# A linear-attention and mixture-of-experts kernel on one core: the first batch's path, the order of its loads and the table that sets the order of the work are changed

## The chip, the core and the metric

The kernel runs on one core of a Trainium2 chip. A core has TensorE (PE in the profile, PEld for its weight loads), VectorE (DVE), ScalarE (ACT), GpSimd (POOL) and SyncE (SP), which here only issues transfers. Each engine takes its instructions in the order in which they are written, and semaphores make one wait for another. The metric is the time of one execution in microseconds of the device, the median of several runs.

## The reference

For 8 batches, 8 heads, 576 tokens and a head size of 64 in fp32, a linear attention with a normalised output feeds four attention experts; each token uses the two experts with the highest gate.

```python
kv = einsum('bhsd,bhse->bhde', k, v)                       # 64 x 64 for each head
o = einsum('bhsd,bhde->bhse', q, kv)
x = o / sqrt(mean(o * o, -1) + 1e-6) * g_norm              # heads side by side: 576 x 512
logits = x @ w_gate                                        # 4 experts, two are kept
for e in range(4):
    q, k, v = x @ wq[e], x @ wk[e], x @ wv[e]              # 512 -> 64
    a = softmax(causal(q @ k.T / 8))                       # 576 x 576
    out += gate[e] * (a @ v @ wo[e])                       # 64 -> 512
```

## The kernel before, in words

The eight batches run through the same chain of tasks. A task has a short name and the batch as its first index. `lk`, `lv` and `lq` load k, v and q of a batch: k and v each in two pieces of 640 and 512 KB (batch 0 in four), q in two halves of 576 KB. `kv` are 40 products in four groups of ten (line 374), `kvc` and `kvm` copy and rearrange their result, `qc` turns q on DVE (line 390), `out` are the products with q (line 401, two halves of tokens), `oc` copies them out of PSUM and `sq` squares them. `SS` sums the squares over each head and `L` makes the logits with the unscaled output (both line 426). `ln`, `rs`, `na`, `nb`, `nc` make 1/sqrt of the sums with one Newton step, `pa` to `pd` split that into two bf16 parts, `sp` spreads them over the partitions with eight small products for each half (line 542), and `xm` multiplies, which gives x (line 552). Then `qp` and `kp` project x onto two experts at a time (line 576), `sc` makes scores (594), `exp` and `msk` the softmax's numerators, `v` the values (561), `pv` their product (623), `rc`, `iv`, `osc` scale, `dt` or `ot` transpose, `y` is the last projection (668), `yc` copies it and `st` stores it. Set-up work goes beside this: `lw` loads the weights for q, k, v in six pieces of 256 KB, in rows of 256 bytes, `ws` scales them by g_norm into place, `z` clears pads, `es` makes the matrix that `sp` multiplies with.

The order of all tasks is written out: `ORDER` is a table of two-character codes into the list that `names` makes, `ENGINE` gives the engine or the queue of each task, and `BANKS` its PSUM banks. The main loop (line 709) emits the tasks in that order, so each engine's and each queue's order follows from it. `ZEROS` puts products of zeros ahead of a task (line 704): 8, 2, 3, 2 and 1 of them, up to batch 1. `GATE` has one digit for each load: a digit n other than 0 makes the load wait until the load n places earlier has landed. A load also waits until its buffer is free: k, v and q have two buffers each, so the loads of a batch wait for the products, or for q's turn, two batches earlier. Almost all loads and stores are issued by SP, one after the other; seven of batch 0's ten are issued by ACT.

The order of the tasks sets what PE does between two loads: PE has in hand what the loads up to there allow, and waits at the first task in its list that lacks data.

Of the kernel before, what the change touches and what calls it, by code (L numbers as in the profile page):

```python
# [53 lines left out]
ENGINE = (
    "AVSGSGVVGVVGGGGVGVGGVGVGGGVVVVVVSSSSSSAGAAGVGVGGGVSASASAASAAASAAPPPPAVAVVVVPPAAVGAAAAPPAAGVVAVAVVVVVVVVVVAVGVV"
    "VPPVVVVPVPAPAPAPAPAPAPAPAGGGGPVGVPVGVSPAPVPAPAPAPAGGGGPVVVPVGVSPASPVSPASPVSPVSSSSSSSPPPPAAGVVVVPPAAVAAGVAPPAAV"
    "VVGVAVVVVVVVVVVAVVVVVPPVVVVPAPAPVPVPAPAPAPAPAGGGGPVVVPVGVSPAPAPAPAPAPAGGGGPVVVPVVVSPASPASPASPASPVSSSSSSSPPPPVG"
    "GVVVVPPAGAGAAVGPPAAGVVVVVVVVVVVVVVGAVVVVGPPVVVVPAPVPAPVPAPAPAPAPAGGGGPVGVPVVVSPAPAPAPAPAPAGGGGPVGVPVGVSPVSPASP"
    "ASPASPASSSSSSSPPPPVGVVVVVPPVGAGAAAAPPAAVVVGVVVVVGVVVVVVAVVVVGPPVVVVPAPAPVPAPAPAPAPAPAGGGGPVVVPVVVSPVPAPAPAPAPA"
    "GGGGPVVVPVVVSPASPASPASPVSPVSSSSSSSPPPPAGAVVVVPPVGAGAGVGPPAAGVVGVGVVVVVVVVVVAVVVVGPPVVVVPVPVPAPAPVPAPAPAPAGGGGP"  # L60
    "VGVPVVVSPAPAPAPAPAPAGGGGPVGVPVGVSPVSPASPASPASPASSSSSSSPPPPVVGVVVVPPVGAGAGAGPPAAGVVGVVVVVVVVVVVGAVGVVVPPVVVVPVP"
    "APAPAPAPAPAPAPAGGGGPVGVPVVVSPVPAPAPAPAPAGGGGPVVVPVVVSPASPASPVSPASPVSSSSSSSPPPPVGGVVVVPPVGAGAGAGPPAAVVVVVGVVVVV"
    "VVVVGAVVVVGPPVVVVPVPAPAPVPVPAPAPAPAGGGGPVVVPVVVSPVPAPAPAPAPAGGGGPVGVPVGVSPASPASPASPASPASSSSSSSPPPPAVAVVVVPPVGA"
    "GAGAAPPAAVVVGVGVVVVVVVVVGAVGVVVPPVVVVPAPAPVPVPAPAPAPAPAGGGGPVVVPVVVPVPVPAPAPAPAPAGGGGPVVVPVVVPVPASPVSPASPASPAS"
)
# [684 lines left out]
```

## Time and profile before

| what | value |
|---|---|
| median of 3 runs | 211.37 us (210.36 to 211.82) |
| the profiled execution | 210.57 us |
| its span, from the first to the last instruction | 208.8 us |
| PE busy | 189.7 us (91%), of it 17.1 us products of zeros |
| PEld, DVE, ACT, POOL busy | 147.6, 145.6, 120.5, 82.5 us |
| chain that ended last | PE 68%, DMA 11%, DVE 11%, ACT 4%, issue 3% |
| read from HBM, written | 30.42 MB, 9.44 MB |
| granted TensorE clock, mean | 0.978 |

The profiled execution lies 1.8 us above its span and 0.8 us below the median. PE is busy nearly all the time from the 43rd microsecond on, so what matters is when that state is reached, and whether the loads keep up with it. A busy PE is not a PE at its peak: products that wait for one another inside the engine count as busy.

### The profile page before, as it was taken

What the parts mean: (1) busy time and instruction counts of PE and PEld (TensorE: products, weight loads), DVE (VectorE), ACT (ScalarE), POOL (GpSimd) and SP (SyncE); (2) the same over time, 40 slices, a digit from 0 to 9 for tenths busy, and PEclk for the clock granted to TensorE, in tenths of its full rate; (3) what the DMA queues carried; (4) which work ended last, traced back from release to release, by engine and by line L of the source; (5) the groups of instructions that cost most, each with busy time, mean ns of one, the idle gap of its engine ahead of it and who ended that gap; (6) DMA issues with size and microseconds to landing.
All of it is one profiled execution on the core that took longest, in us unless ns stands there. A gap on an engine that the chain in (4) does not pass through costs nothing.

```text
span 208.8 us, 7252 instructions
## 1 busy us (share of the span) xinstructions
PE 189.7 (91%) x3003; PEld 147.6 (71%) x3018; DVE 145.6 (70%) x368; ACT 120.5 (58%) x206; POOL 82.5 (40%) x184
## 2 busy tenths in 40 slices
PE   7937979599999799999999899999999999999990
PEld 3327456497988587787778688877877888788750
DVE  3023194889769987786997897549986889856660
ACT  2001164954766717665669538657756664789871
POOL 3000053750885822105735550736615252145400
PEclk9995899999999999999999999999999999999997
DMA  5996997999998986859959876601510930353886
GB/s 154 332 374 212 354 161 181 294 173 326 269 337 283 316 289 130 267 189 353 308 159 184 274 250 168 209 8 38 199 36 11 194 91 0 90 153 110 143 296 248
DMA packets 41536, 42.61 MB, mean 204 GB/s; under 512 B 17696, under 2 KB 35104, under 8 KB 41504
## 3 DMA queue, kind: packets, MB, share of 16 engines
q1 hardware_dynamic: 39792, 39.47, 66.7%
q10 hardware_dynamic: 1648, 2.69, 3.7%
q8 instruction: 23, 0.38, 0.7%
q14 instruction: 9, 0.07, 0.1%
q0 software_dynamic: 64, 0.00, 0.1%
HBM read 30.42 MB, written 9.44 MB: 191 GB/s over the span
## 4 chain that ended last, share of the span: by engine, by line
PE 68%; DMA 11%; DVE 11%; ACT 4%; issue 3%; POOL 0%; ACTq 0%; POOLq 0%; DVEq 0%
PE ps L576 14%; PE ps L374 9%; PE ps L594 8%; DMA k_b<-in_k_dram 8%; PE ps L401 7%; PE ps L561 7%; PE ps L426 6%; PE ps L668 6%; PE ps L623 5%; PE ps L704 3%; DMA v_b<-in_v_dram 3%; DVE qT L390 2%; DVE osc L643 2%; PE ps L542 2%; DVE inv L639 1%
## 5 line engine op out<-in xcount | busy, mean ns | idle before, releaser
L605 ACT ACTIVATE PT<-ps 128x1024 bf16<-128x1024 f32 (+1 forms) x64 | 50.9, 835 | 18.4 <-PE ps L594 15.3
L611 POOL TENSOR_SCALAR_AFFINE_SELECT PT<-PT 128x256 bf16<-128x256 bf16 (+1 forms) x80 | 29.2, 387 | 30.2 <-ACT PT L605 29.8
L419 POOL TENSOR_TENSOR sq<-o_sb 128x576 f32<-128x576 f32 x22 | 25.0, 1153 | 32.5 <-DVE jh L310 24.7
L390 DVE STREAM_TRANSPOSE qT<-q_b 128x576 f32<-128x576 f32 x32 | 23.6, 757 | 13.5 <-DMA q_b<-in_q_dram 13.4
L552 DVE TENSOR_TENSOR xT<-o_sb,ps 128x640 fp32r<-128x640 f32 x32 | 24.9, 816 | 3.8 <-PE ps L542 3.5
L374 PE MATMUL ps<-v_b,k_b 128*64 128x64 f32 x640 | 22.9, 232 | 4.7 <-DMA k_b<-in_k_dram 3.6
L374 PEld LDWEIGHTS ps<-v_b,k_b 128*64 128x64 f32 x640 | 21.4, 146 | 7.6 <-DMA k_b<-in_k_dram 3.6
L561 PE MATMUL ps<-wv_r,xT 128*128 128x256 f32 x160 | 23.9, 292 | 0.6 <-DVE osc L643 0.5
L594 PE MATMUL ps<-qTp,kT 64*128 64x64 f32 (+4 forms) x192 | 22.5, 339 | 0.2
L561 PEld LDWEIGHTS ps<-wv_r,xT 128*128 128x128 f32 x160 | 20.4, 188 | 2.7 <-DVE osc L643 0.9
L223 ACT COPY y<-ps 128x512 f32<-128x512 f32 (+1 forms) x29 | 15.7, 559 | 9.6 <-PE ps L668 7.4
L576 PE MATMUL ps<-xT,wq_r 128*128 128x288 f32 x128 | 20.0, 302 | 0.0
L576 PE MATMUL ps<-xT,wk_r 128*128 128x288 f32 x128 | 19.8, 299 | 0.0
L623 PEld LDWEIGHTS <-PT 128*128 128x128 bf16 x480 | 16.7, 97 | 4.4 <-issue 1.2
L704 PE MATMUL ps<-zeros 128*128 128x512 f32 (+1 forms) x32 | 17.1, 677 | 2.7 <-DVE zeros L250 1.1
L223 ACT COPY o_sb<-ps 128x576 f32<-128x576 f32 x22 | 13.5, 638 | 10.2 <-PE ps L401 10.1
L668 PE MATMUL ps<-wo_b,OT 128*128 128x512 bf16 (+1 forms) x81 | 18.3, 343 | 0.6 <-issue 0.2
L623 PE MATMUL ps<-vext,PT 128*128 128x65 bf16 x480 | 18.6, 193 | 0.2
L576 PEld LDWEIGHTS ps<-xT,wq_r 128*128 128x128 f32 x128 | 17.5, 188 | 1.3 <-issue 0.9
L576 PEld LDWEIGHTS ps<-xT,wk_r 128*128 128x128 f32 x128 | 17.7, 188 | 1.0 <-ACT o_sb L223 0.4
L594 PEld LDWEIGHTS ps<-qTp,kT 64*128 64x128 f32 x192 | 14.3, 185 | 5.7 <-issue 2.0
L643 DVE TENSOR_TENSOR osc<-ps,inv 128x256 bf16<-128x256 f32 (+1 forms) x32 | 15.3, 484 | 2.8 <-POOL inv L639 2.2
(110 smaller groups left out, 264.0 us busy)
## 6 DMA issues: line engine op xcount, KB each, us to landing
out_dram<-y SPq DMA_DIRECT2D x32, 256.0 KB, 2.8
q_b<-in_q_dram SPq DMA_DIRECT2D x14, 576.0 KB, 5.8
v_b<-in_v_dram SPq DMA_DIRECT2D x7, 640.0 KB, 7.4
k_b<-in_k_dram SPq DMA_DIRECT2D x7, 640.0 KB, 7.0
k_b<-in_k_dram SPq DMA_DIRECT2D x7, 512.0 KB, 6.5
v_b<-in_v_dram SPq DMA_DIRECT2D x7, 512.0 KB, 5.9
q_b<-in_q_dram ACTq DMA_DIRECT2D x2, 576.0 KB, 7.5
out_dram<-y SPq DMA_DIRECT2D x16, 64.0 KB, 2.1
```

Source lines behind the costliest of these rows:

```text
L223: return nc.scalar.copy(dst, src)
L374: nc.tensor.matmul(p_kv[Dh * t : Dh * t + Dh, j, hh, :], lhsT=kb_[b % NK][:, h, n, :], rhs=vb_[b % NK][:, h, n, :], start=(n == 0), stop=( ...
L390: nc.vector.transpose(qT_[0][:, hh, j * n : (j + 1) * n].rearrange("p j h i -> p (j h i)"), qb_[b % 2][:, hh, j * n : (j + 1) * n, :].rear ...
L419: inst = ew("sq", b, u, p).tensor_tensor(out=dst, in0=src, in1=src, op=mult)
L552: nc.vector.tensor_tensor(out=view(xT_[b % 2]), in0=view(ob_[b % 2]), in1=two("sp", b, u, p)[:, :, 0:320].rearrange("p s (m j) -> p m s j" ...
L561: nc.tensor.matmul(one("v", b, i)[:, n * 256 : (n + 1) * 256], lhsT=xT_[b % 2][:, c, blk * P : (blk + 1) * P], rhs=w_r["v"][:, c].rearrang ...
L576: nc.tensor.matmul(bank_in((nm + "p", b, pr), s)[:, 0:HALF], lhsT=w_r[nm][:, c, 2 * pr : 2 * pr + 2, :].rearrange("p e f -> p (e f)"), rhs ...
L594: nc.tensor.matmul(bank_in(("sc", b, pr, j), el)[:, o : o + hi - lo], lhsT=kT_[(2 * b + pr) % 3][pp, kb * P : (kb + 1) * P], rhs=qTp_[(2 * ...
L605: nc.scalar.activation(PT[:, :, d0 : d0 + o], two("sc", b, pr, j)[:, :, 0:o], ACTF.Exp, scale=scale)
L611: nc.gpsimd.affine_select(out=d, in_=d, compare_op=AluOpType.is_ge, fill=0.0, base=0, pattern=[[0, 2], [1, w]], channel_multiplier=-1)
L623: nc.tensor.matmul(p_O[:, (2 * n + el) * (Hd + 1) : (2 * n + el + 1) * (Hd + 1)], lhsT=PT[:, el, col : col + P], rhs=vx_[b % 2][:, kb, 2 * ...
L668: nc.tensor.matmul(p_y[o * nq : (o + 1) * nq, 0:w], lhsT=OT_[b % 2][:, pr, s0 : s0 + nq], rhs=wo_b[:, pr, o * w : (o + 1) * w], start=(pr ...
```

## The change

Batch 0 gets a path of its own. Its k and v are loaded in two pieces each as in the other batches, its first half of q is the very first load, and its second half comes in two pieces of 288 KB. `sq` of batch 0 reads PSUM on ACT and no longer the copy; its sums `SS` are split into two halves, the second of them `SS2`. `pa` to `pd` are dropped for batch 0: `sp` multiplies the fp32 result of `nc` with a matrix in fp32 that the new task `e32` makes in the buffer `y_[2]`. Of the four `xm` of batch 0 two go to POOL, which reads a copy that the new task `xs` makes on ACT. Only 9 products of zeros are left, ahead of the first `kv`. The loads of g_norm and of the gate's weights become two tasks, issued by ACT. The output of the last two batches is copied into the buffers of k and v, and a store of the last 64 tokens is one transfer, not two. All four tables are new, so the tasks of every batch stand in another order, and many have another engine.

```diff
-ZEROS = {('kv', 0, 0, 0): 8, ('kv', 0, 1, 0): 2, ('out', 0, 1): 3, ('kv', 1, 1, 1): 2, ('out', 1, 1): 1}
+ZEROS = {('kv', 0, 0, 1): 9}
...
-    "01000P0E0v0u0R0U090x0t080A0z0s0B0+17100y0w120-07192z2+131A11141615181C1J1K2-"
...
+    "010A0v0t0D060714130N0P0Q0R050C0U0u0r0s0z020J0S040803000w0x152w0E160I0-"
...
 GATE = (
-    "440006650500463600435646400660633303055345542523520320300236"
+    "000000065544044055564506006553456430300023036240420420606"
 )
...
+    def e32():
+        for a in range(2):
+            ew("e32").tensor_scalar(
+                out=esel_f[:, :, a, :], in0=jj[:, 4 * a : 4 * a + 4, 0].unsqueeze(2).to_broadcast([P, NCH, Dh]),
+                scalar1=-0.5, scalar2=None, op0=mult,
+            )
...
-    def lq(b, hh):
-        return queue("lq", b, hh).dma_start(
-            qb_[b % 2][:, hh].rearrange("p j d -> p (j d)"), q[b, 4 * hh : 4 * hh + 4].rearrange("g (i j) d -> (g i) (j d)", j=NJ)
+    def lq(b, hh, *half):
+        js = slice(half[0] * NJ // 2, (half[0] + 1) * NJ // 2) if half else slice(0, NJ)
...
     def square(b, u, p):
+        if b == 0:
+            src = two("out", b, u, p)[:, :, 0:HALF].rearrange("p c (j i) -> p c i j", j=NJ)
+            dst = sq_[0][:, 2 * p : 2 * p + 2, u * HALF : (u + 1) * HALF].rearrange("p c (i j) -> p c i j", j=NJ)
+            return other_half(nc.scalar.activation(dst, src, ACTF.Square), ("sq", b, u, p))
...
     def ss_mm(b):
-        sums(("SS", b), w_ss, sq_[0])
+        sums(("SS", b), w_ss, sq_[0], range(NCH if b else 2))
+
+    def ss_rest(b):
+        sums(("SS", b), w_ss, sq_[0], range(2, NCH))
...
-                    lhsT=esel[rows, c].rearrange("p a d -> p (a d)"),
-                    rhs=flat(rb["rc"][b % 2])[rows], start=True, stop=True, skip_group_check=True, tile_position=(32 * s, 0),
+                    lhsT=(esel if b else esel_f)[rows, c].rearrange("p a d -> p (a d)"),
+                    rhs=flat(rb["rc"][b % 2] if b else ssl["rstd"][b % 2])[rows], start=True, stop=True, skip_group_check=True, tile_position=(32 * s, 0),
...
+        spread_r = two("sp", b, u, p)[:, :, 0:320] if b or not p else sp_copy(u)
+        ew("xm", b, u, p).tensor_tensor(
+            out=view(xT_[b % 2]), in0=view(ob_[b % 2]), in1=spread_r.rearrange("p s (m j) -> p m s j", j=32), op=mult
+        )
+
+    def sp_copy(u):
+        return sq_[0][:, 2 * u : 2 * u + 2, 0:320]
+
+    def xs(_, u):
+        nc.scalar.copy(sp_copy(u), two("sp", 0, u, 1)[:, :, 0:320])
...
     def y_copy(b, i):
-        y_of[b, i] = y_[y_next[0] % NY]
-        y_next[0] += 1
+        if b >= B - NK:
+            t = (vb_, kb_)[b - B + NK][(B - NK) % NK]
+            y_of[b, i] = t[:].rearrange("p h j d -> p (h j d)")[:, i * D : (i + 1) * D]
...
```

What the tables do is read from the instructions in their order. The head of PE's list, before (zeros are line 704, `kv` line 374, `out` line 401):

```order
L704 MATMUL ps<-zeros 128x512 x8
L374 MATMUL ps<-v_b_81,k_b_79 64x64 x10
L704 MATMUL ps<-zeros 128x256 x2
L374 MATMUL ps<-v_b_81,k_b_79 64x64 x30
L704 MATMUL ps<-zeros 128x512 x3
L401 MATMUL ps<-qT_89,kvs_85 64x288 x8
L401 MATMUL ps<-qT_89,kvx_87 64x288 x8
L401 MATMUL ps<-qT_89,kvs_85 64x288 x8
```

and now (zeros line 734, `kv` 386, `out` 413, `SS`, `SS2` and `L` 442, `sp` 561, `kp` and `qp` 601; v_b_81 and k_b_79 are the buffers of batch 0, v_b_82 and k_b_80 those of batch 1):

```order
L734 MATMUL ps<-zeros 128x512 x9
L386 MATMUL ps<-v_b_81,k_b_79 64x64 x40
L413 MATMUL ps<-qT_89,kvs_85 64x288 x8
L413 MATMUL ps<-qT_89,kvx_87 64x288 x8
L413 MATMUL ps<-qT_89,kvs_85 64x288 x8
L413 MATMUL ps<-qT_89,kvx_87 64x288 x8
L442 MATMUL ps<-sq_92,w_ss 32x160 x16
L442 MATMUL ps<-o_sb_90,wg 32x160 x16
L561 MATMUL ps<-rstd_95,y_154 128x160 x16
L386 MATMUL ps<-v_b_82,k_b_80 64x64 x40
L601 MATMUL ps<-xT_133,wk_r 128x288 x8
L601 MATMUL ps<-xT_133,wq_r 128x288 x8
```

Before, the products of zeros stand between the groups of batch 0, and batch 1's `kv`, `out`, `SS` and `L` stand ahead of the first projection; now batch 0 goes through to `sp` first, then `kv` of batch 1, and the projections `kp` and `qp` of two experts follow at once, ahead of `out` of batch 1.

The head of SP's list of loads, before (v_b0, k_b0, q_b0 are the buffers of batch 0, those with a 1 of batch 1, PT0 to PT2 hold the weights; the other loads of batch 0 are on ACT's queue):

```order
L352 DMA v_b0_81<-in_v_dram 64x4x256 x2
L352 DMA k_b0_79<-in_k_dram 64x4x320
L352 DMA v_b1_82<-in_v_dram 64x8x320
L352 DMA k_b1_80<-in_k_dram 64x8x256
L352 DMA v_b1_82<-in_v_dram 64x8x256
L352 DMA k_b1_80<-in_k_dram 64x8x320
L364 DMA q_b1_84<-in_q_dram 128x1152 x2
L256 DMA wg_in_65<-in_moe_w_gate_dram 64x4x4
L253 DMA g8_64<-in_g_norm_dram 64x1
L352 DMA k_b0_79<-in_k_dram 64x8x320
L328 DMA PT1_144<-in_moe_wk_dram 64x16x64
L328 DMA PT0_143<-in_moe_wq_dram 64x16x64 x2
```

and now (the two pieces of k of batch 0 are on ACT's queue):

```order
L375 DMA q_b0_83<-in_q_dram 128x1152
L362 DMA v_b0_81<-in_v_dram 64x8x256
L362 DMA v_b0_81<-in_v_dram 64x8x320
L375 DMA q_b0_83<-in_q_dram 128x576 x2
L362 DMA v_b1_82<-in_v_dram 64x8x256
L375 DMA q_b1_84<-in_q_dram 128x1152
L362 DMA k_b1_80<-in_k_dram 64x8x320
L338 DMA PT1_144<-in_moe_wk_dram 64x16x64
L362 DMA v_b1_82<-in_v_dram 64x8x320
L362 DMA k_b1_80<-in_k_dram 64x8x256
L338 DMA PT0_143<-in_moe_wq_dram 64x16x64
L375 DMA q_b1_84<-in_q_dram 128x1152
```

Before, SP's first three pieces are of batch 0 and the next ones of batch 1; now all of batch 0 stands first, and weights for k and q stand among the loads of batch 1. The list goes on in both with batch 2, the weights for v, and batches 3 and 4.

## Rows read from the trace of the kernel before

**Rows 1.** The chain of waits that ended last, first 45 us (start and length in us, what ran; "DMA" is a transfer that was waited for, x the number of records).

```profile
2.74 6.67 DMA v_b<-in_v_dram
9.48 6.06 DMA k_b<-in_k_dram
...
16.50 3.48 PE ps L374 x60
20.00 0.38 ACT kvs L223
20.43 3.70 PE ps L704 x6
24.13 1.24 PE ps L401 x32
...
27.32 1.99 PE ps L704 x4
29.32 2.48 PE ps L374 x80
31.80 1.22 PE ps L426 x32
...
40.36 2.38 PE ps L426 x64
42.74 3.38 PE ps L576 x24
```

**Rows 2.** The timeline of the first products of zeros (start and length in us, engine, line, operation, shapes; PE are the products, PEld their weight loads, one for each record).

```profile
1.12 9.12 PE L704 MATMUL ps<-zeros 128*128 128x512 f32 x16 [1.12 <-DVE zeros L250]
...
5.34 0.19 PEld L704 LDWEIGHTS ps<-zeros 128*128 128x128 f32 x1 [0.30 <-issue]
5.77 0.19 PEld L704 LDWEIGHTS ps<-zeros 128*128 128x128 f32 x1 [0.24 <-issue]
```

**Rows 3.** Busy time of the engines in stretches of the start (us from the span's start, then length, PE, PEld, DVE, ACT, POOL busy with counts, granted clock, mean busy share of the DMA engines, GB/s).

```profile
10.00:15.00 5.00, 2.11 (x25) 1.37 (x24) 1.12 (x5) 0.00 (x0) 0.00 (x0) 1.00 1.06 373
15.00:20.00 5.00, 3.47 (x60) 3.31 (x60) 1.44 (x2) 0.00 (x0) 0.00 (x0) 0.54 0.66 204
20.00:25.00 5.00, 4.57 (x38) 2.16 (x46) 1.28 (x4) 0.96 (x3) 0.00 (x0) 0.78 1.03 372
...
30.00:35.00 5.00, 5.00 (x128) 3.70 (x132) 2.20 (x6) 1.70 (x5) 1.46 (x5) 1.00 0.59 112
```

**Rows 4.** The same view in longer stretches, up to the landing of the last piece of k of batch 4 (79.34 us).

```profile
2.74:20.00 17.26, 12.84 (x99) 7.59 (x97) 3.04 (x8) 0.00 (x0) 0.00 (x0) 0.87 0.90 301
20.00:60.00 40.00, 36.02 (x614) 26.69 (x615) 26.86 (x55) 23.16 (x42) 18.62 (x30) 0.97 0.99 261
60.00:79.34 19.34, 17.59 (x368) 14.56 (x366) 17.99 (x49) 10.77 (x21) 11.79 (x25) 1.00 0.88 291
20.00:50.00 30.00, 26.02 (x462) 18.19 (x462) 20.43 (x45) 16.37 (x32) 12.10 (x21) 0.96 1.00 243
50.00:60.00 10.00, 10.00 (x156) 8.49 (x157) 6.43 (x11) 6.79 (x10) 6.52 (x9) 1.00 0.95 313
```

**Rows 5.** The chain of waits later on: blocks of products, and the two transfers waited for ahead of `kv` of batch 4 (line 374 at 79.48).

```profile
52.73 4.44 PE ps L576 x32
57.17 2.21 PE ps L401 x64
...
68.65 4.95 DMA k_b<-in_k_dram
73.61 5.73 DMA k_b<-in_k_dram
79.48 2.55 PE ps L374 x80
...
90.35 0.54 PE ps L623 x18
...
104.71 2.55 PE ps L561 x20
...
137.73 0.38 PE ps L623 x12
```

**Rows 6.** The timeline of ACT and DVE in the normalisation of batch 0: a square, then `ln`, `rs`, `nc`, and the last of `pa` to `pd`.

```profile
26.06 0.68 ACT L417 ACTIVATE sq<-o_sb 128x576 f32<-128x576 f32 x1
...
33.09 0.39 ACT L442 ACTIVATE root<-ps,eps_t 128x160 f32<-128x160 f32 x1 [0.22 <-PE ps L426]
...
33.51 0.34 ACT L445 ACTIVATE rstd<-root 128x160 f32<-128x160 f32 x1
...
34.91 0.33 DVE L458 SCALAR_TENSOR_TENSOR rstd<-root,rstd 128x160 f32<-128x160 f32 x1
...
38.07 0.94 DVE L473 SCALAR_TENSOR_TENSOR rc<-rb,m_b,part 128x160 bf16<-128x160 bf16 x1
```

**Rows 7.** Groups of instructions by shape (busy us, mean ns of one, idle time before them and its releasers): the squares on POOL, `xm` on DVE, the scaling of weights on POOL.

```profile
L419 POOL TENSOR_TENSOR sq<-o_sb 128x576 f32<-128x576 f32 x22 | 25.0, 1153 | 32.5 <-DVE jh L310 24.7 <-ACT o_sb L223 7.0 <-DVE o_sb L226 0.8
L552 DVE TENSOR_TENSOR xT<-o_sb,ps 128x640 fp32r<-128x640 f32 x32 | 24.9, 816 | 3.8 <-PE ps L542 3.5 <-ACT wq_r L338 0.2
...
L340 POOL TENSOR_SCALAR wk_r<-PT,g 64x512 fp32r<-64x512 f32 x2 | 3.1, 1562 | 0.2
```

**Rows 8.** The chain of waits: the last copy of an output block ahead of the last stores.

```profile
203.45 0.28 ACT y L223
```

More of the change, by code (lines that the diff above doesn't have):

```diff
@@ L53 @@
+    "EqEwErEsGSGTGsEtExEyEuF0GtH4H5G+EvF1F2H1H6G-H0H2GuGvGxGwGyGzH3"
 )
 ENGINE = (
[L55 to L58, printed above, removed]
@@ L89, in names @@
     for b in range(nb):
-        out += [(m, b, part, par) for part in (r2 if b == 0 else (2,)) for par in r2 for m in ("lk", "lv")]
-        out += [("lq", b, hh) for hh in r2]
+        out += [(m, b, part, par) for part in (2,) for par in r2 for m in ("lk", "lv")]
+        out += [("lq", b, hh) for hh in r2] if b else [("lq", 0, 0), ("lq", 0, 1, 0), ("lq", 0, 1, 1)]
         out += [("kv", b, hh, j) for hh in r2 for j in r2] + [("kvc", b)] + [("kvm", b, t) for t in r2]
@@ L94, in names @@
         out += [("out", b, u) for u in r2] + [(m, b, u, p) for u in r2 for p in r2 for m in ("oc", "sq")]
-        out += [(m, b) for m in ("L", "SS", "ln", "rs", "na", "nb", "nc", "pa", "pb", "pc", "pd", "gm", "gtr", "lg")]
+        out += [] if b else [("SS2", 0), ("xs", 0, 0), ("xs", 0, 1)]
+        out += [(m, b) for m in ("L", "SS", "ln", "rs", "na", "nb", "nc") + (("pa", "pb", "pc", "pd") if b else ()) + ("gm", "gtr", "lg")]
         out += [(m, b) for m in ("g1", "g2", "g3", "g4", "g5", "sh", "ex", "mk", "gt", "den", "rd", "gate")]
@@ L213 @@
     y_ = sbt([P, D], FP32, "y", NY)
+    esel_f = y_[2][:].rearrange("p (c a d) -> p c a d", c=NCH, a=2)
     stage = {
@@ L250, in cz, with cg, cw @@
         nc.vector.memset(zeros[:], 0.0)
-    def cg(hh):
-        queue("cg", hh).dma_start(g8[hh * Dh : (hh + 1) * Dh, :], g_norm.unsqueeze(1))
-    def cw(hh):
-        queue("cw", hh).dma_start(
-            wg_in[hh * Dh : (hh + 1) * Dh], moe_w_gate[hh * D // 2 : (hh + 1) * D // 2, :].rearrange("(c p) e -> p c e", p=Dh)
-        )
+    def cg():
+        queue("cg").dma_start(g8[:], g_norm.unsqueeze(0).unsqueeze(2).to_broadcast([2, Dh, 1]))
+    def cw():
+        for hh in range(2):
+            rows = moe_w_gate[hh * D // 2 : (hh + 1) * D // 2, :].rearrange("(c p) e -> p c e", p=Dh)
+            queue("cw").dma_start(wg_in[hh * Dh : (hh + 1) * Dh], rows)
     def scale_g():
@@ L420, in square, with sums @@
         other_half(inst, ("sq", b, u, p))
-    def sums(key, w, src):
-        for c in range(NCH):
+    def sums(key, w, src, chunks=range(NCH)):
+        for c in chunks:
             for s in range(4):
@@ L683, in store @@
         w = D * nq // P
[L684 to L685 removed]
+        n = P // nq
+        dst = out[b, s0 : s0 + nq, :].rearrange("q (o w) -> o q w", o=n)
+        queue("st", b, i).dma_start(dst, y_of[b, i][:, 0:w])
     emit = dict(
[L688 removed]
+        at=at, cz=cz, cg=cg, cw=cw, g8=scale_g, cs=cs, z=z, wg=wgate, id=ident, idb=idb, j1=j1, j2=j2, es=es, e32=e32, ma=ma, mb=mb,
         lw=lw, ws=ws, lwo=lwo, wo=wo, lk=lk, lv=lv, lq=lq, kv=kv, kvc=kv_copy, kvm=kv_move, qc=q_turn, out=out_mm, oc=o_copy, sq=square,
[L690 to L691 removed]
+        L=l_mm, SS=ss_mm, SS2=ss_rest, ln=ln, rs=rs, na=newton_a, nb=newton_b, nc=newton_c, pa=pa, pb=pb, pc=pc, pd=pd, gm=gm, gtr=gtr,
+        lg=lg, g1=g1, g2=g2, g3=g3, g4=g4, g5=g5, sh=sh, ex=ex, mk=mk, gt=gt, den=den, rd=rd, gate=gate, sp=spread, xs=xs, xm=xm,
         v=v_mm, vc=v_copy, qp=lambda b, pr: proj("q", b, pr), kp=lambda b, pr: proj("k", b, pr),
```

91 lines of the change are left out of this document (46 added, 45 removed).

## The prediction

> **What bounds the kernel now.** I read the page's table first: PE is busy 91% of the span, so the question is where the other 9% and the products of zeros lie. The chain of waits tells of the start [rows 1]: two transfers up to 15.54 us, `kv` of batch 0 from 16.50 to 19.98, a copy of 0.38, then 3.70 us of zeros that stand ahead of `out` in PE's list and hold it back, and so on through batch 1's `kv` and sums until the first projection at 42.74. The reader is to see that 42.7 us pass before PE has work without end, and that zeros (3.70, 1.99) stand on that chain themselves.
>
> The second view is the stretches [rows 4]. The DMA engines are busy 0.90, 0.99 and 0.88 of the time up to 79.34 us, where the last piece of k of batch 4 lands. The chain names two transfers of k ahead of `kv` of batch 4, which starts at 79.48 [rows 5]. So up to there the transfers set the pace, though PE finds other work meanwhile (17.6 of 19.3 us busy in the last of these stretches). From 79.48 to the end of the span 129.3 us are left, and PE is their bound.
>
> **The change, part by part: the head.** `kv` of batch 0 needs its k, v and, ahead of them in the list, half of q: 2.95 MB. At a rate of 0.34 MB per us of busy DMA (329 in 50 to 60, 331 in 60 to 79, 352 in 10 to 15 us: GB/s over share [rows 3, 4]) and the share of 0.90 of the first stretch it lands 9.6 us after the first stretch's start at 2.74, at 12.4 us; the bounds are 10.7 at the 373 GB/s of 10 to 15 us and 15.5 as before. The 9 products of zeros don't hold it: 16 records end at 10.24, two more take 0.43 each [rows 2], so 11.1. Then, step by step: `kv` 2.48 to 14.9; its copy 0.38, the rearranging about 0.6 and the rest of a half of `out` about 0.6 (half of its 1.24) to 16.5 [rows 1]; four squares on ACT at 0.68 to 19.2; `SS2`, half of 1.22, to 19.9; `ln` to `nc` 2.15 (33.09 to 35.24) to 22.0 [rows 6]. The way from there to 39.01, the end of `pd`, 3.8 us [rows 6], is gone. No row shows `sp` in fp32: it lies between half of an `SS` (0.61: as many columns and records, four at a time) and the same 16 records one after the other (160 of 512 columns of 0.43, 2.1 in all); I take 0.61, the nearer kind. The copy `xs` costs about 0.7, and POOL's two multiplies 1153 x 640/576 = 1.28 each [rows 7], against 0.82 on DVE: x is whole at about 26.0. Meanwhile PE does `kv` of batch 1, whose loads (6.75 MB, with one of the weights) land at about 24.4; with 2.48 it ends at 26.9. So the first projection starts near 27 us, 15.8 earlier, with 4.6 us of PE work less behind it (`out`, `L`, `SS` of batch 1).
>
> **The transfers.** This is where most of those 15.8 us are lost. The loads of the weights cost more than their bytes: in 20 to 50 us the share was 1.00 and 243 GB/s were moved [rows 4], 7.29 MB or 21.4 us at 0.34; the 8.6 us over are those of the six weight loads, 1.4 each. For `kv` of batch 4 the new list needs k and v of five batches (11.80 MB), q of four (4.72) and the six weights (1.57), 18.09 MB: 53.2 + 8.6 = 61.8 us of busy DMA. The same sum for before, 21.04 MB, gives 70.5; measured were 0.90 x 17.26 + 0.99 x 40 + 0.88 x 19.34 = 72.2. The new gates leave four to six loads in flight in most of this part; the old ones, with 3 in places, went with a share of 0.59 in 30 to 35 us and of 0.66 in 15 to 20 [rows 3]. I take a share of 0.98, near the 0.99 of 20 to 60 us: 63.1 + 2.7 = 65.8 us. The bounds are 1.06 as in 10 to 15 us (61.0) and 0.88 as in 60 to 79 us (72.9).
>
> PE alone would be there sooner: from the first projection to `kv` of batch 4 the list holds about 30 us of products, which gives 57. Half-way stands `v` of batch 0, which needs the last weights: 12.19 MB, 45.4 us of DMA time at that share, landed at 48.1, scaled at 49.7 (1.56 on POOL [rows 7]); PE would reach it at 42.0. From there 14.9 us of products lead to `kv` of batch 4, at 64.6, within a microsecond of the transfers. So nothing in the head costs anything until it is 8 us worse than above: the wait for the loads covers the longer `sp`, POOL's multiplies, and the loads of weights that DVE's `ws` tasks wait for ahead of copies of batch 1.
>
> **What is left then.** The 129.3 us from `kv` of batch 4 on, and what the new list puts behind it: `SS` of batch 3 (1.22), its `out` (2.21), four `pv` (1.84), two blocks of `v` of batch 1 (2.04, 16 of 20 records in 2.55), scores 0.2 [rows 1, 5], together 7.5: 136.8 us. The rest goes together at nothing: six squares fewer on POOL and six more on ACT (6.9 and 4.1 us) lie under PE, which bounds this part; the own buffers for the last outputs and the single stores of 64 tokens lie in the last 5.4 us after 203.45 [rows 8], where they may give or cost 1 us, since five stores of a batch must still go out. DVE, 18.0 of 19.3 us busy in 60 to 79 [rows 4], is next should PE run faster.
>
> The sum: 65.8 + 136.8 = 202.6 of span, and the 1.8 us around it as before, 204.4, against the profiled 210.57. That execution was 0.8 below the median, so **205.2 us** to compare with 211.37.
>
> **A rule against it.** In 15 to 20 us the granted clock was 0.54, so nearly all of it at the level of 1.2 GHz, after PE had been busy 2.11 of the five microseconds before; at 20 to 25 it was 0.78, then 1.00 [rows 3]. Now PE has gaps in its head and no zeros to fill them. The Trainium skill (TensorE: Matmul & The Clock Gate, section Why this matters for your kernels) warns that idle gaps between bursts of matmuls send the array back to its lower clock; by that rule the sum would be the third rival's. The trace agrees that the clock falls, and shows that it came back while the engine was kept waiting now and then; I keep 205.2.
>
> **Rivals.** First, more: the DMA engines stay as busy as in 10 to 15 us, 1.06, and `kv` of batch 4 starts at 61.0; then 200.4. Against it: before had no more than 0.99 over 20 to 60. Second, little: the transfers gain nothing by their new order, because loads still wait for buffers that PE frees late and the share stays at the 0.90 of the first stretch: 68.7 + 2.7 = 71.4, then 210.8. For it: before reached 0.88 in 60 to 79 us with its gates of 3, and the new gates have 3 there too. Third, slower: the clock. A record of `kv` took 58 ns in 16.5 to 20 us (3.48 for 60) and 31 at the full clock (2.48 for 80) [rows 1], 1.87 times as long. Were PE at 1.2 GHz from the end of the first `kv` to `v` of batch 0, 23.4 us of products (`out` to `kv` of batch 1 8.3, then 15.1) would take 20.4 more: `v` starts at 62.4 and not 49.7, and the end is 12.7 later, 217.9. It decides from 7.7 us added on (the cover), and makes the kernel slower by over 1% from 16 us on, that is 18 us of work at half clock. Against it: in 30 to 35 us the clock was 1.00 [rows 3].
>
> **The numbers.** Chances: forecast 0.58 (its own range 202 to 208.5), more 0.12, little 0.20, clock 0.10. A measurement of this kernel tells about 1% from no change, so faster is below 209.3 and slower above 213.5. The forecast and the first rival are faster; of the second 0.07 are, 0.11 are the same and 0.02 slower; the third is slower: 0.77, 0.11, 0.12. The range of 199 to 212 leaves out the clock and the ends of the first two rivals, about 2 in 10.
>
> **What would show it.** In the new profile: the first projection near 27 us; a DMA share near 0.98 from 5 us to 60; PE waiting for transfers ahead of `kv` of batch 2, `v` of batch 0 or `kv` of batches 3 and 4, the last near 66; from there 137 us to the end with PE busy as before. I am wrong if the clock stands at its lower level for more than a few microseconds after 15 us, if the share stays near 0.9, or if PE, after `kv` of batch 4, waits for other engines where it did not before.

## The result and the profile after

The changed kernel takes 214.39 us, median of 20 runs (211.72 to 217.11); the kernel before, on the same chips, 211.31 (210.36 to 216.23). The ratio is 1.010, interval 1.007 to 1.013: slower by 1%, where 205.2 us was forecast. Ratios are taken without the slow executions, those over 1.5% above the quickest of their kernel (here 8 of the 20), and so this one lies below the quotient of the two medians, 1.015. The profiled execution is the quickest of the twenty, 211.72 us, with a span of 210.0; the spread of the others comes up again below.

The chain of waits of the changed kernel, its first 50 us, answers to [rows 1] (line 386 is `kv`, 601 the projections, 413 `out`, 586 `v`):

```profile
2.86 11.08 DMA g<-in_g_norm_dram
...
14.12 0.79 DVE qT L402 x2
...
17.41 8.18 DMA k_b<-in_k_dram
...
25.72 4.07 PE ps L386 x80
29.79 2.55 PE ps L601 x16
32.34 1.26 PE ps L413 x32
...
34.41 9.03 DMA q_b<-in_q_dram
...
48.26 1.64 PE ps L586 x12
```

The first projection starts at 29.79 us instead of 42.74, and `v` of batch 0 at 48.26. The stretches answer to [rows 3, 4]:

```profile
20.00:25.00 5.00, 2.31 (x60) 1.73 (x52) 3.91 (x8) 2.71 (x5) 1.35 (x1) 1.00 1.17 263
25.00:30.00 5.00, 4.28 (x82) 4.19 (x83) 1.34 (x3) 0.89 (x2) 1.93 (x3) 0.66 1.14 193
30.00:35.00 5.00, 5.00 (x84) 3.85 (x84) 3.41 (x6) 3.65 (x7) 4.32 (x6) 1.00 1.00 304
```

```profile
2.74:20.00 17.26, 15.60 (x205) 8.68 (x207) 6.95 (x18) 5.08 (x10) 5.21 (x16) 1.00 1.06 329
20.00:60.00 40.00, 34.70 (x668) 28.39 (x661) 27.06 (x63) 23.63 (x40) 15.90 (x26) 0.96 1.06 292
```

More is moved than before in the same time (329 and 292 GB/s for 301 and 261), and `kv` of batch 4 starts at 64.54. So far the head is as forecast. What is not is the end. PE's last group of products, in the timeline:

```profile
194.12 2.98 PE L693 MATMUL ps<-wo_b,OT 128*128 128x512 bf16 x17
```

It ends at 197.10, 6.6 us earlier than before, where line 668's last group ends at 203.66:

```profile
200.72 2.94 PE L668 MATMUL ps<-wo_b,OT 128*128 128x512 bf16 x14
```

But the span ends 1.2 us later. The stretches behind that last product show what runs there: nothing but stores, and those on few engines.

```profile
196.00:198.00 2.00, 1.05 (x5) 0.29 (x3) 1.83 (x3) 0.58 (x1) 0.00 (x0) 1.00 0.99 381
198.00:200.00 2.00, 0.00 (x0) 0.00 (x0) 0.00 (x1) 0.00 (x0) 0.00 (x0) 1.00 0.50 155
200.00:202.00 2.00, 0.00 (x0) 0.00 (x0) 0.00 (x0) 0.00 (x0) 0.00 (x0) 0.60 0.88 274
202.00:204.00 2.00, 0.00 (x0) 0.00 (x0) 0.00 (x0) 0.00 (x0) 0.00 (x0) 0.50 0.45 160
204.00:206.00 2.00, 0.00 (x0) 0.00 (x0) 0.00 (x0) 0.00 (x0) 0.00 (x0) 0.50 0.13 49
206.00:208.00 2.00, 0.00 (x0) 0.00 (x0) 0.00 (x0) 0.00 (x0) 0.00 (x0) 0.50 0.13 50
```

The second column from the right is the mean busy share of 16 DMA engines, the last GB/s. A share of 0.13 is two of sixteen (0.125), and 49 of the 381 GB/s of the first line are about two sixteenths (47.6). The view gives only the mean over the sixteen; read this way, two engines work for four microseconds and fourteen have nothing left.

Set against the sum of the prediction, whose 129.3 and 136.8 us contained the 5.1 from the last product to the end of the span:

| stage | forecast | measured |
|---|---|---|
| start to `kv` of batch 4 | 65.8 | 64.5 |
| from there to the end of the last product | 131.7 | 132.6 |
| from there to the end of the span | 5.1 | 12.9 |
| span | 202.6 | 210.0 |

The whole miss of the profiled execution stands in the third line; the median lies another 2.7 us above that execution. (The expectations below count 13.3 us there, from 196.7, where the chain passes to the last copy.)

### The profile page after: what moved, and what is told of

Read it like the earlier page. It is cut to its first block, busy times and chain, and to the rows that moved or that the text cites. A ratio compares the mean times of both kernels' runs of the same rounds, so it can differ in the third digit from the quotient of the medians.

```text
span 210.0 us, 7256 instructions
## 1 busy us (share of the span) xinstructions
PE 185.8 (88%) x3009; PEld 145.9 (69%) x3020; DVE 141.1 (67%) x359; ACT 125.8 (60%) x216; POOL 77.1 (37%) x187
## 3 DMA queue, kind: packets, MB, share of 16 engines
q1 hardware_dynamic: 39454, 40.31, 66.4%
## 4 chain that ended last, share of the span: by engine, by line
PE 67%; DMA 13%; DVE 8%; issue 2%; ACT 1%; POOL 1%; SPq 0%; ACTq 0%; POOLq 0%; DVEq 0%
PE ps L601 15%; PE ps L586 8%; PE ps L386 8%; PE ps L619 7%; PE ps L648 7%; PE ps L413 7%; PE ps L442 7%; PE ps L693 7%; DMA g<-in_g_norm_dram 5%; DMA q_b<-in_q_dram 4%; DMA k_b<-in_k_dram 4%; DVE qT L402 2%; DVE kvx L229 2%; PE ps L561 1%; ACT PT L630 1%
## 5 line engine op out<-in xcount | busy, mean ns | idle before, releaser
L572 DVE TENSOR_TENSOR xT<-o_sb,ps 128x640 fp32r<-128x640 f32 x30 | 23.4, 814 | 6.3 <-PE ps L561 6.2
L386 PE MATMUL ps<-v_b,k_b 128*64 128x64 f32 x640 | 21.9, 232 | 3.0 <-DMA k_b<-in_k_dram 3.0
L435 POOL TENSOR_TENSOR sq<-o_sb 128x576 f32<-128x576 f32 x16 | 18.4, 1159 | 10.5 <-ACT o_sb L226 7.0
L619 PE MATMUL ps<-qTp,kT 64*128 64x64 f32 (+4 forms) x192 | 21.2, 338 | 0.0
L601 PE MATMUL ps<-xT,wq_r 128*128 128x288 f32 x128 | 20.8, 304 | 0.0
L601 PE MATMUL ps<-xT,wk_r 128*128 128x288 f32 x128 | 20.6, 304 | 0.2 <-ACT PT L630 0.2
L648 PEld LDWEIGHTS <-PT 128*128 128x128 bf16 x480 | 16.3, 97 | 3.7 <-issue 1.0
L668 DVE TENSOR_TENSOR osc<-ps,inv 128x384 bf16<-128x384 f32 (+1 forms) x32 | 15.2, 486 | 2.8 <-POOL inv L664 2.3
L413 PE MATMUL ps<-qT,kvs 32*64 32x288 f32 x256 | 14.6, 415 | 1.4 <-ACT kvs L226 0.5
L226 ACT COPY o_sb<-ps 128x576 f32<-128x576 f32 x19 | 11.6, 644 | 6.4 <-PE ps L413 6.4
L413 PE MATMUL ps<-qT,kvx 32*64 32x288 f32 x256 | 13.6, 403 | 1.1 <-DVE kvx L229 1.1
```

Of the source, the lines that this page charges most:

```text
L386: nc.tensor.matmul(p_kv[Dh * t : Dh * t + Dh, j, hh, :], lhsT=kb_[b % NK][:, h, n, :], rhs=vb_[b % NK][:, h, n, :], start=(n == 0), stop=( ...
L413: nc.tensor.matmul(p_o[Dh * hh : Dh * hh + Dh, 0:HALF], lhsT=kvx_[b % 2][rows, hh, :] if m else kvs_[b % 2][rows, g % 2, hh, :], rhs=qT_[0 ...
L435: inst = ew("sq", b, u, p).tensor_tensor(out=dst, in0=src, in1=src, op=mult)
L572: ew("xm", b, u, p).tensor_tensor(out=view(xT_[b % 2]), in0=view(ob_[b % 2]), in1=spread_r.rearrange("p s (m j) -> p m s j", j=32), op=mult)
L601: nc.tensor.matmul(bank_in((nm + "p", b, pr), s)[:, 0:HALF], lhsT=w_r[nm][:, c, 2 * pr : 2 * pr + 2, :].rearrange("p e f -> p (e f)"), rhs ...
L619: nc.tensor.matmul(bank_in(("sc", b, pr, j), el)[:, o : o + hi - lo], lhsT=kT_[(2 * b + pr) % 3][pp, kb * P : (kb + 1) * P], rhs=qTp_[(2 * ...
```

## The experiments

Ratios are to the kernel before, run on the same chip, with 95% intervals. The times are those of each one's profile, one execution that can lie 1 to 2 us from the run's median, in us: the starts of `kv` of batches 1 and 4, the end of the last product, and as "end" the rest of the span. A yardstick is the kernel of e1, run again beside other kernels for comparison.

| run | ratio | `kv` 1 | `kv` 4 | last product | end |
|---|---|---|---|---|---|
| changed kernel | 1.010 [1.007, 1.013] | 25.7 | 64.5 | 197.1 | 12.9 |
| e1, two stores | 0.975 [0.968, 0.982] | 26.9 | 67.2 | 200.8 | 6.2 |
| e2, before, one store | 1.025 [1.020, 1.031] | - | 79.0 | 203.4 | 10.7 |
| e3, all on SP | 1.017 [1.011, 1.022] | 28.0 | 66.9 | 199.5 | 12.8 |
| e4, y ring | 1.020 [1.013, 1.026] | 28.1 | 67.6 | 202.7 | 10.8 |
| e13, two by columns | 1.032 [1.018, 1.046] | 26.3 | 65.0 | 199.0 | 14.2 |
| e5, two stores again | 0.976 [0.971, 0.982] | 26.7 | 66.4 | 199.1 | 6.2 |
| e6, zeros at gaps | 0.977 [0.972, 0.982] | 26.5 | 63.9 | 196.8 | 6.5 |
| e7, more load | 0.991 [0.986, 0.997] | 30.8 | 71.5 | 205.3 | 6.4 |
| e8, less load | 0.978 [0.973, 0.982] | 26.4 | 65.8 | 198.6 | 6.2 |
| e9, two stores, y ring | 0.983 [0.978, 0.988] | 27.0 | 67.8 | 201.2 | 6.1 |
| e10, one store early | 0.987 [0.980, 0.993] | 27.5 | 66.3 | 200.9 | 6.3 |
| e11, projection first | 0.987 [0.982, 0.992] | 32.6 | 66.9 | 199.8 | 6.2 |
| e12, zeros again | 0.987 [0.983, 0.991] | 27.6 | 67.7 | 200.6 | 6.9 |
| e14, yardstick | 0.993 [0.987, 0.998] | 27.1 | 65.7 | 203.0 | 6.2 |
| e15, one store early again | 0.987 [0.980, 0.994] | 26.2 | 67.2 | 200.9 | 6.2 |
| e16, q of batch 4 earlier | 0.981 [0.975, 0.988] | 27.0 | 66.4 | 199.1 | 6.1 |
| e17, yardstick | 0.985 [0.981, 0.989] | 27.9 | 67.1 | 199.7 | 6.2 |
| e18, and copies on ACT | 0.981 [0.975, 0.986] | 26.1 | 66.1 | 197.5 | 6.5 |

**What makes the end long.** The theory is the store of a block of 64 tokens, which the change issues as one DMA of 2 x 64 rows. e1 takes that back:

```diff
-        n = P // nq
-        dst = out[b, s0 : s0 + nq, :].rearrange("q (o w) -> o q w", o=n)
-        queue("st", b, i).dma_start(dst, y_of[b, i][:, 0:w])
+        for o in range(P // nq):
+            queue("st", b, i).dma_start(out[b, s0 : s0 + nq, o * w : (o + 1) * w], y_of[b, i][o * nq : (o + 1) * nq, 0:w])
```

> The changed kernel with the store of a block of 64 tokens as two DMAs again, one for each half of the columns. Theory of the two engines (the one DMA of 2 x 64 rows goes over two of the 16 DMA engines, which then end last): the 13.3 us from the last product (196.7) to the end of the span (210.0) shrink to the 5.1 us of the kernel before, so the span is about 202 us and the ratio to the kernel before about 0.965; the DMA share in the last 6 us is high and falls at once, instead of the long foot at 47 to 52 GB/s. Rival, the own buffers: the end stays at about 210 and the ratio at 1.01. Rival, the three stores on ACT's queue: also 1.01. Rival, PE: the last product itself comes later, and the ratio is between.

e2 makes the opposite edit in the kernel before:

> The kernel before with nothing changed but the store of 64 tokens, now one DMA as in the change. Theory of the two engines: the two of them carry 112 KB more for the blocks of 64 tokens of batches 6 and 7, at 23 to 26 KB per us and engine (the foot's 47 to 52 GB/s halved) 4.3 to 4.9 us, so the end comes about 4.5 us later, at 213, ratio 1.02. Rivals (own buffers, ACT's queue): no change, ratio 1.00, or a gain of 0.5 us from the issue saved.

e3 turns three letters of `ENGINE`:

```diff
- st 7 1: A, st 7 3: A, st 7 4: A
+ st 7 1: S, st 7 3: S, st 7 4: S
```

> The changed kernel with its three stores of batch 7 that go over ACT's queue on SP's as all others. Theory of the two engines: nothing changes but 1 to 2 us of issue, ratio 1.00 to 1.02, the foot at 47 to 52 GB/s stays. Rival, ACT's queue: the stores of both queues no longer take turns on the same engines and the last ones land 2 to 3 us after their issue, ratio below 0.98.

e4 sends every output to the ring `y_`:

```diff
-        if b >= B - NK:
-            t = (vb_, kb_)[b - B + NK][(B - NK) % NK]
-            y_of[b, i] = t[:].rearrange("p h j d -> p (h j d)")[:, i * D : (i + 1) * D]
-        else:
-            y_of[b, i] = y_[y_next[0] % NY]
-            y_next[0] += 1
+        y_of[b, i] = y_[y_next[0] % NY]
+        y_next[0] += 1
```

> The changed kernel without its own buffers for the last outputs (the ring of y buffers for all batches). Theory of the two engines: the foot stays, and since stores on the two engines now free the buffers late, copies of y wait for them: ratio 1.01 to 1.03. Rival, the own buffers (reads of the wider k and v buffers are slow): the end comes 5 us earlier, ratio 0.98.

e1 makes the kernel 2.5% faster than the kernel before and the end 6.2 us; e2 makes the kernel before 2.5% slower (5.3 us for the 4.5 expected) with its last product where it was (203.4 for 203.7). Neither the queue (e3) nor the own buffers (e4) make the long end: without them it is 12.8 and 10.8 us. But the buffers decide how it comes about. In e2, where all outputs go through the ring, the last copy waits until a narrow store gives its buffer back:

```profile
199.77 6.62 DMA out_dram<-y
...
206.50 0.59 ACT y L223
```

ACT waits 3.2 us there; in e4 the copies wait 5.0 us in all for stores out of the ring, and PE in turn for copies. Of the 7.8 us by which the end of the changed kernel is longer than the end before, e1 takes 6.7 back; 1 us or more stays in every kernel with two stores, without the own buffers too (e9, below), and no run shows from what. The last 14 us of e1 show the other shape of an end, in the view of the DMA queues (40 slices, busy share in tenths and GB/s):

```profile
DMA  9900345599999999999999999989999999500000
GB/s 222 194 13 0 85 103 126 167 380 375 392 369 386 369 386 375 398 351 421 369 392 375 380 263 205 284 316 377 340 398 375 392 375 380 217 18 0 0 0 0
```

It stays full and falls at once. Whether the form of the DMA or the mere number is at fault was asked by e13, which issues two, but cut by columns, so that each again has 2 x 64 rows:

```diff
...
+        for c in range(2):
+            cols = slice(c * w // 2, (c + 1) * w // 2)
+            queue("st", b, i).dma_start(dst[:, :, cols], y_of[b, i][:, cols])
```

> The changed kernel with two DMAs for a block of 64 tokens, each of 2 x 64 rows again but of half the length (512 bytes), cut by columns and not by halves of the partitions. Theory (the leading 2 of the form puts it on two engines): the foot at the end stays, at 0.12 to 0.14 of DMA share and no more than 50 GB/s, the end comes 12 us or more after the last product, ratio 1.01 or more. Rival (one DMA too few, any two would do): as the two stores, ratio 0.975 to 0.985, and 6 us after the last product.

```profile
DMA  9949910189211111011119999993111111000000
GB/s 375 281 89 315 299 67 22 28 304 383 81 38 26 47 56 35 20 37 42 44 47 332 364 366 379 372 364 103 45 54 45 47 56 47 35 29 6 0 0 0
```

Two DMAs of that form are no better than one, and it is not the number: it is the leading 2. (Their rows are also half as long, which this run doesn't separate; but the one DMA, with rows as long as in e1, has the same share.) The view of e13 (199.2 to 213.2 us, slices of 0.35) shows a second thing. The foot of 20 to 56 GB/s appears twice, and between the two stand six slices at 332 to 379, in which full blocks are stored. They were not issued earlier, as e13's timeline of the two queues shows (start and length of the issue; SP first, then ACT):

```profile
199.29 3.52 SPq L720 DMA_DIRECT2D out_dram<-v_b  x2
202.92 3.63 SPq L716 DMA_DIRECT2D out_dram<-k_b  x2
```

```profile
200.45 5.85 ACTq L716 DMA_DIRECT2D out_dram<-k_b  x2
```

Line 720 is the narrow form, 716 a full block. Issuing two full blocks took 3.63 us, and on ACT's queue 5.85 passed until two were out; in e1's timeline it is 1.09 for the last two:

```profile
201.03 1.09 SPq L714 DMA_DIRECT2D out_dram<-k_b  x2
```

So such a DMA seems to delay not only its own bytes: issues behind it stall while the share is at 0.1. That they wait for it is inferred from the order in time. The changed kernel has the same hole, smaller (a share of 0.50 in 198 to 200 us).

The Trainium skill (DMA: Bandwidth & Descriptors, section Rules for kernel authors) says that the size of the outermost dimension, where it is below 16, limits on how many of the 16 engines a whole DMA can run. The trace agrees with it to the number: 2 outermost, a share of 0.13.

**Does it cost before the end?** e10 and e15 are one kernel: one DMA for batches 0 to 4, two for the rest.

```diff
+        if b < 5:
+            dst = out[b, s0 : s0 + nq, :].rearrange("q (o w) -> o q w", o=n)
+            queue("st", b, i).dma_start(dst, y_of[b, i][:, 0:w])
+            return
```

> The changed kernel in which the blocks of 64 tokens of batches 0 to 4 keep the one DMA, and only those of batches 5 to 7 are stored as two. Theory (two engines; it costs only where the stores end last, at the end): as with two stores throughout, ratio 0.972 to 0.98, the end 6 us after the last product. Rival (the two engines slow the loads of later batches too): 0.005 or more above that, with later kv of batches 5 to 7.

> One store for the blocks of 64 tokens of batches 0 to 4 and two for batches 5 to 7, beside its yardstick. Theory (the form costs only at the end): the same ratio as the yardstick within the intervals (0.006). Rival (two slow engines hold later loads and the stores in the middle up): 0.008 or more above it.

0.987 twice, and the yardstick beside the second is e14, the kernel of e1 again:

> The kernel with two stores a third time, as the yardstick of the run beside it: ratio 0.974 to 0.987.

It came out at 0.993, above its range, so no cost can be seen. e2's last product agrees that PE didn't wait for such stores; with the ring in the changed kernel (e4) it did, by way of the copies, for 1.5 us in all near the end. The yardstick's own scatter is the next finding. Four runs of one kernel gave 0.975, 0.976, 0.993 and 0.985, so differences of under 1% between kernels that were not run side by side tell nothing here.

**What bounds the head?** With the end mended, the prediction's step on the transfers can be tried. The yardstick of e6, e7 and e8:

> The same kernel as in the run with two stores, once more, as the yardstick of the runs beside it: span 202 to 207, ratio to the kernel before 0.97 to 0.98. Kv of batch 4 at 64 to 67 us, from there 132 to 134 us to the last product, then 5 to 6 us.

e6 and e12 put zeros at two waits:

```diff
-ZEROS = {('kv', 0, 0, 1): 9}
+ZEROS = {('kv', 0, 0, 1): 9, ('kv', 1, 0, 1): 2, ('kv', 2, 1, 0): 1}
```

> The kernel with two stores, and two products of zeros ahead of kv of batch 1 and one ahead of kv of batch 2, where PE waits for loads and its clock then falls to 0.6 to 0.8 in a stretch of 5 us. Theory of the prediction (the transfers decide up to kv of batch 4, PE's own pace in between is covered): kv of batch 1 takes 2.5 instead of 4.0 us, but kv of batch 4 and the end don't move, the same ratio as the yardstick within 0.3%. Rival, the clock: PE is the bound of the head, kv of batch 4 comes 1.5 to 3 us earlier and the ratio falls by 0.007 to 0.014. Worse: the zeros hold kv back, up to 1 us.

> The kernel with the zeros at the gaps once more, for a second trace and a narrower interval. If its granted clock from 25 to 45 us is whole again and kv of batch 1 to kv of batch 4 takes 37.4 us again (38.8 to 40.3 without the zeros), the clock's share is shown; a ratio of 0.977 again says that the timed runs don't gain by it, 0.970 or less that they do.

e7 reads 0.59 MB once more beside `lq 1 0`, into the `OT` buffers; e8 cuts the loads of q of batch 2:

```diff
+        if (b, hh) == (1, 0):
+            for x in range(2):
+                spare = OT_[x][:].rearrange("p a s -> p (a s)").bitcast(FP32)[:, 0 : NJ * Dh // 2]
...
+        if b == 2:
+            js = slice(0, 1)
```

> The kernel with two stores, and 0.59 MB read once more, into a buffer that nothing reads before batch 0's outputs (two DMAs beside a half of q of batch 1). Theory of the prediction (the transfers set the pace up to kv of batch 4): 0.59 MB at 0.34 MB per us of busy DMA and a share of 1.06 is 1.6 us, and the end comes 1.6 us later, ratio 0.008 above the yardstick. Rival, PE or the other engines bound the head: no change.

> The kernel with two stores, in which both halves of q of batch 2 are read with one column block of 18 (the rest of the buffer is left out, so batch 2 works on old data): 1.11 MB less. Theory of the prediction: 1.11 MB is 3.1 us of the transfers, and kv of batch 4 comes up to 3.1 us earlier, until products stand in the way (PE alone would be there 8 us earlier by the prediction): ratio 0.010 to 0.015 below the yardstick. Rival, the head is bound by PE and its copies: below 0.3% of change.

e11 changes the order (and the banks with it; `ws q 1 1` goes ahead of `kp 0 1` too):

```diff
+ lw k 1, lw q 1
  lv 1 2 1
...
+ kp 0 1, qp 0 1
  kv 1 0 1, kv 1 1 0, kv 1 1 1, kv 1 0 0
- kp 0 1, qp 0 1
```

> The kernel with two stores, in which the first projections of k and q of batch 0 stand ahead of kv of batch 1, and their weights are loaded ahead of its k and v. Theory (up to kv of batch 1 the transfers are the bound, from there PE and its clock): the first projection starts at about 27 us instead of 30 to 31, since its x is whole at 26.7, kv of batch 4 comes 1.5 to 3 us earlier, ratio 0.007 to 0.014 below the two stores. Rival of the prediction (the transfers set the pace up to kv of batch 4): no change. Worse: kv of batch 1 and out of batch 1 come so late that what hangs on them holds PE, ratio up to 0.01 above.

0.59 MB more, ahead of `kv` of batch 1, costs 4.1 us there and 5.1 at `kv` of batch 4 in the profile, 0.015 in the ratio (3.2 us) and 5.5 us in the median of all twelve executions: at least twice the expected 1.6. So the transfers bind up to `kv` of batch 1. 1.11 MB less gives nothing in the ratio, where 0.010 to 0.015 was expected. But its trace doesn't show that the transfers have no part behind that point. The loads that e8 cuts stand behind those of k of batch 2, and for these `kv` of batch 2 waited 2.67 us in this execution, against 0.63 in e5; from there PE went on without waiting for loads (a line of PE's timeline, then the stretch up to `kv` of batch 4):

```profile
42.85 2.55 PE L388 MATMUL ps<-v_b,k_b 128*64 128x64 f32 x80 [2.67 <-DMA k_b<-in_k_dram]
...
42.85:65.84 22.99, 22.81 (x431) 18.93 (x431) 18.59 (x45) 14.34 (x25) 6.99 (x15) 1.00 0.99 327
```

That is 23.0 us from `kv` of batch 2 to that of batch 4, where e5 took 25.2. So in this one trace PE is the bound of that stretch once there is less to load, and the loads had a part in it before; the ratios don't show the gain. The zeros do hold the granted clock at 1.00 in 25 to 30 us (0.66 in the changed kernel), in both traces:

```profile
25.00:30.00 5.00, 4.16 (x89) 3.43 (x88) 1.19 (x3) 1.57 (x3) 2.34 (x5) 1.00 1.17 205
```

(this one is e6). From `kv` of batch 1 to that of batch 4 e6 needs 37.4 us, but e12, at the same clock, 40.1, as long as the kernels with two stores and no zeros (38.6 to 41.0): its chain goes over q of batch 2, which lands at 45.64, and `kv` of batch 4 waits 0.8 us for a load. The ratios, 0.977 beside a yardstick of 0.976, and 0.987 in a series without one, show no gain. So the clock's fall in the head costs nothing that these runs can tell from scatter. In e11 the projection starts at 27.9, but `kv` of batch 0 comes 1.6 us later and `kv` of batch 4 stands at 66.9; the ratio, 0.987 without a yardstick beside it, shows no gain either.

**The own buffers**, with the stores mended (the edit of e4 in e1's kernel):

> The kernel with two stores, without the own buffers for the outputs of batches 6 and 7 (the ring of y buffers for all). The prediction's price of the own buffers: they may give or cost 1 us. So the ratio is 0.972 to 0.982, the last product comes up to 1 us later, the end 6 us after it. Rival: with the stores mended, the ring holds copies of y back and PE waits; the last product comes over 2 us later, ratio 0.985 and more.

0.983, between the yardsticks, and an end of 6.1 us: with two stores they neither give nor cost anything that shows.

**What still lies above the forecast.** In e14's trace `kv` of batch 5 comes 23.2 us after that of batch 4, in most others 18.7. Its chain goes over `lq 4 0`, issued at 64.73:

```profile
64.73 8.32 DMA q_b<-in_q_dram
```

`out` of batch 4 took 7.4 us there; 4.0 in the changed kernel, 2.2 for an `out` in the kernel before. Part of it is the clock: while PE waited it was busy 0.79 of 3 us, and then the granted clock was 0.50 for 5 us (the last 44 products of `out` took 3.17 us, and 1.79 at the full clock in e16):

```profile
76.00:79.00 3.00, 0.79 (x11) 0.19 (x4) 2.97 (x2) 0.15 (x1) 3.00 (x7) 0.85 0.96 371
79.00:84.00 5.00, 4.94 (x69) 3.04 (x70) 2.16 (x5) 1.28 (x2) 0.17 (x1) 0.50 0.75 250
```

e16 issues that load earlier (with the gates moved along), e17 is the yardstick:

```diff
  lq 4 1
+ lq 4 0
  lwo o 1, lk 5 2 0
- lq 4 0
```

> The kernel with two stores, in which the second half of q of batch 4 is read right after the first, ahead of the first half of the output weights and of a piece of k of batch 5 (0.92 MB, 2.7 us at 0.34 MB per us). Theory (out of batch 4 waits on DVE's turning of that half): it lands 2 to 3.5 us earlier, out of batch 4 takes 2.2 to 3 us instead of 4 to 7, kv of batch 5 comes 18 us after kv of batch 4 instead of 18.7 to 23.2, the ratio is 0.005 to 0.015 below the yardstick. Rival: k of batch 5, now later, or the slow copies of kv on DVE hold out of batch 4 as long: no change.

> The kernel with two stores once more, beside it: ratio 0.975 to 0.993, out of batch 4 taking 4 us or more.

In e16 q landed at about 68.7 us instead of e17's 71.1 (issue and time to landing added), `out` of batch 4 still took 4.0 us, and the ratio, 0.981 beside 0.985, is within the intervals: the rival held. DVE's timeline in e16 (line 224 is the copy that moves kv between partitions) and POOL's beside it:

```profile
71.17 2.10 DVE L397 STREAM_TRANSPOSE qT<-q_b 128x576 f32<-128x576 f32 x3 [1.76 <-PE ps L408]
...
74.19 3.58 DVE L224 COPY kvx<-kvs 32x128 f32<-32x128 f32 x2
```

```profile
74.11 1.15 POOL L430 TENSOR_TENSOR sq<-o_sb 128x576 f32<-128x576 f32 x1
75.21 0.65 POOL L631 TENSOR_SCALAR_AFFINE_SELECT PT<-PT 64x128 bf16<-64x128 bf16 x2
75.83 1.14 POOL L430 TENSOR_TENSOR sq<-o_sb 128x576 f32<-128x576 f32 x1
76.93 1.00 POOL L631 TENSOR_SCALAR_AFFINE_SELECT PT<-PT 128x256 bf16<-128x256 bf16 x3
```

By the chain the first copy runs from 74.19 to 75.33, and POOL's first square ends at 75.26; the second, from 75.37 to 77.78, outlasts two masks, a square and more masks. e18 gives these two copies to ACT:

```diff
- kvm 4 0: V
+ kvm 4 0: A
```

(its letter in `ENGINE`), on top of e16.

> The kernel with q of batch 4 earlier, and the two copies that move kv of batch 4 between partitions on ACT and not on DVE. Theory (these copies stand still while POOL works: 3.54 us for what takes 0.43 alone): they take 0.3 us each on ACT, out of batch 4 takes 2.2 to 2.5 us instead of 4.0, kv of batch 5 comes 17 us after kv of batch 4 instead of 18.7, the ratio is 0.008 below the run with q earlier alone (0.981), 0.970 to 0.977. Rival (DVE's order or q hold out of batch 4 all the same, or ACT's copies of kT and v are late by as much): no change, 0.981.

The chain of e18 shows the copies at 0.30 us each and `out` of batch 4 (line 408) at 2.13:

```profile
72.43 0.30 ACT kvx L221
...
72.74 0.30 ACT kvx L221
...
75.85 2.13 PE ps L408 x64
```

`kv` of batch 5 comes 17.4 us after that of batch 4, 1.3 less than in e16 and e17; the median is 206.18 us (e16 207.48, e17 207.56), the ratio 0.981, above the 0.970 to 0.977 expected, and the intervals don't tell it from e16's. So the 1.3 us show in the trace and not in the ratio. The median is the lowest of all kernels tried, but on a chip where the kernel before was quick too (210.44): it beats that by 2%, interval 1.4 to 2.5, no more than e1 and e5 do.

## Why the prediction was wrong

**The single stores: the step that failed.** "The own buffers for the last outputs and the single stores of 64 tokens lie in the last 5.4 us [...] where they may give or cost 1 us." The end grew by 7.8 us in the profiled execution, and the stores are 6.7 of it (e1); the own buffers cost nothing that shows (e9). I counted DMAs and bytes and not how many of the 16 engines a DMA gets, so the term had no mechanism in it that could cost more. [Rows 8] showed only an end with stores of the old form; the new form stood in the diff. No rival held it either, and the range ended 2.4 us below the median.

**The head: near, and covered.** `kv` of batch 0 started at 11.5 (12.4 forecast), `sp` began at 21.95 (22.0) and took 1.37 us, not 0.61, and `kv` of batch 1 began at 25.7, so that the first projection came at 29.8 instead of 27: `kv` of batch 1 waited for its k and then took 4.07 us, not 2.48, at the lower clock. Also unforeseen: `g_norm`, in the chain above, held the turning of q behind it on DVE until 14.12. `v` of batch 0 came at 48.3 (49.7).

**The transfers: the right number, half the reason.** `kv` of batch 4 at 64.5, and 63.9 to 67.8 in all traces of the experiments but e7's and e2's, against 65.8. Two errors cancel here, and that was luck: the share was 1.05 up to there and not 0.98, nearly the first rival's, and by it the DMA engines were busy for 64.9 us in the 61.8 us from 2.74 on, where the sum had 61.8 of busy time in 63.1:

```profile
2.74:64.54 61.80, 54.84 (x905) 40.93 (x903) 38.26 (x89) 31.23 (x54) 21.19 (x42) 0.97 1.05 306
```

Nor did `kv` of batch 4 wait for a transfer in the profiled execution: PE came to it from `v` of batch 0 in 16.3 us (14.9 forecast). e7 shows that ahead of `kv` of batch 1 a load costs at least twice its price, e8 that behind `kv` of batch 2 PE is the bound once there is less to load (23.0 us for 25.2 in e5).

**What is left: right to 1 us** (131.7 against 132.6), though "the rest goes together at nothing" hid 1.8 us at `out` of batch 4 (4.0 for 2.2), of which e18 gives 1.3 back in its trace: copies on DVE that are slow beside POOL. I had looked at how much DVE had to do, not at what works next to it.

**The clock rival** happened in part: 0.66 in 25 to 30 us. As the prediction said, it costs nothing there that shows (e6, e12). In e14 it fell once more, behind `kv` of batch 4 (0.50 in 79 to 84 us), and there it is part of the 4.5 us by which `kv` of batch 5 came later.

**The median.** Four runs of e1's kernel gave 207.5, 207.2, 209.0 and 207.6, 2 to 4 us above the forecast. The profiled execution of the changed kernel was a lucky one: its `kv` of batch 4 stands at 64.5, those of e1, e5, e14 and e17 at 65.7 to 67.2, and q of batch 4 can come late as well. Why the loads of the head take longer in one execution than in another no run here shows.

## What to carry to other kernels

When a change merges DMAs, look at the outermost dimension of the merged one before counting what the issue saves: here a leading 2 left the last stores to 2 of 16 engines and cost what the whole head had won (6.7 us, and 6.6). Read the end of a kernel as a stage of its own, from the last product to the last landing; a gain anywhere ahead passes through it. And an instruction that should take 0.2 us and takes 2.4 is a question about what runs beside it.
